# Order of the first loads: x blocks ahead of the q, k weight pieces, all four weight pieces on ScalarE's queue

## The chip, the core and the metric

The kernel runs on one core of a Trainium2 chip. The core has five engines that work side by side: TensorE (PE in the profile; its weight loads are PEld), VectorE (DVE), ScalarE (ACT), GpSimd (POOL) and SyncE (SP). Each works through its own instructions in order. Transfers between the chip's memory (HBM) and the core's on-chip memory are issued by SP, ACT or POOL as one instruction each, and are then carried out by 16 DMA engines. The metric is the device time of one execution in microseconds (us). Times in the text count from the first instruction of the profiled execution unless it says otherwise.

## What is computed

One transformer layer over 2048 positions of width 512 in bfloat16. Attention has 32 heads of width 16; each position looks at itself and at 7 earlier ones, 2 positions apart. The feed-forward part has a ReLU gate and width 1376.

```python
def _A_ref(x, wqkv, wo):
    H = 32; W, dil = 8, 2
    qkv = (x @ wqkv).reshape(B, S, 3, H, Dh)   # then q, k, v
    idx = pos[:, None] - off[None, :]          # off = arange(W) * dil
    logits = einsum("bhsd,bhswd->bhsw", q, kg) * Dh ** -0.5
    attn = softmax(where(mask, logits, -1e9))
    o = einsum("bhsw,bhswd->bhsd", attn, vg)
    return o @ wo

def _B_ref(x, W_gate, W_up, W_down):
    return (relu(x @ W_gate) * (x @ W_up)) @ W_down

h = x + _A_ref(_layernorm(x), A_wqkv, A_wo)
return h + _B_ref(_layernorm(h), B_W_gate, B_W_up, B_W_down)
```

## The kernel before

The 2048 positions are cut into four chunks of 512, and a chunk into four blocks of 128 positions. Block j of x lies in `x_sm[:, j, :]`, one position to a partition; below it is called xj (x0 to x3 are chunk 0, x4 to x7 chunk 1). The q and k weights lie in `wqk_sb` in four pieces of 128 input rows, `wqk_sb[:, 0..3, :]`, called w0 to w3; each is 256 KB, a block of x 128 KB. The v weights (`wv_sb`), the output weights (`wo_sb`) and the gate weights (`wgu_sb`) follow as larger transfers.

For chunk 0, each block goes its own way into the projections:

- DVE takes the statistics of the block (L467, aggregated by L470).
- ACT makes the reciprocal deviation of it with two activations (L480 logarithm, L484 exponential). They need ACT's function table, which is loaded by L326 in the setup.
- DVE normalizes the block (L515, into a `row` buffer).
- PE transposes it (L544, four matmuls against `identity`).
- ACT (L560), for block 1 DVE (L558), copies the transposed block into a `quad` buffer.
- PE multiplies it with the weights (L585): first the columns of block 0 and then of block 1 against w0 and w1 alone, then all columns against w2 and w3, then blocks 2 and 3.

Before that PE runs 77 matmuls on zeros (L428), and 8 more after the transposes of block 1 (L436). The order of all this on each engine is fixed by a table of ranks (`RANK`), which the change doesn't touch. Only the loads and constants in `setup()` stand outside of the table, ahead of everything else.

In `setup()` a loop issues the first eight loads (L319 to L325), alternating the queues of SP and ACT. On ACT the table load (L326) comes next. After the constants, SP issues w3 (L341), x5 to x7 (L343), the v weights (L344), the x blocks of chunks 2 and 3 (L346), the output weights (L348) and the gate weights (L349). A memset of one element on POOL (L340) stands ahead of w3, so that w3's DMA waits for POOL.

The framework gives each DMA of SP and ACT one of eight completion semaphores, called lanes (DMAHW0 to DMAHW7), in turn, in the order in which it expects the two queues to issue. A DMA that takes a lane again waits first, on the engine that issues it, until the DMA that had the lane has landed.

Of the kernel before, what the change touches and what calls it, by code (L numbers as in the profile page):

```python
# [201 lines left out]
def kernel(  # L202
# [11 lines left out]
    nc = tc.nc  # L214
    Bsz, S, D = A_x.shape
# [23 lines left out]
    BPC = CS // P  # L239
# [26 lines left out]
    wqk_sb = sb.tile([P, NT, 2 * D], BF16, name="wqk_sb")  # L266
# [50 lines left out]
    def setup():  # L317

        w3_r = A_wqkv.rearrange("(dt p) f -> p dt f", p=P)  # L319
        for q, n, j in ((nc.sync, "x", 0), (nc.scalar, "x", 1), (nc.scalar, "w", 0), (nc.sync, "x", 2), (nc.scalar, "w", 1),  # L320
                        (nc.sync, "x", 3), (nc.scalar, "w", 2), (nc.sync, "x", BPC)):
            if n == "x":
                q.dma_start(x_sm[:, j:j + 1, :], x_rows[:, j:j + 1, :])  # L323
            else:
                q.dma_start(wqk_sb[:, j:j + 1, :], w3_r[:, j:j + 1, 0:2 * D])  # L325
        nc.scalar.preload_act_table_set("natural_log_exp_and_others")  # L326
        V.memset(warm[:], 0.0)
        make_identity(nc, identity[:])
        nc.gpsimd.memset(eps_t[:, 0:1], EPS)
        nc.gpsimd.memset(eps_t[:, 1:2], EPS * D * D)  # L330
        nc.gpsimd.iota(ci[:], pattern=[[0, 1]], base=0, channel_multiplier=1)
        nc.gpsimd.iota(sel_i[:], pattern=[[1, H]], base=0, channel_multiplier=0)
        nc.gpsimd.iota(sp_i[:], pattern=[[1, H], [0, DQ]], base=0, channel_multiplier=0)
        nc.gpsimd.iota(sm_i, pattern=[[0, 4], [1, H]], base=0, channel_multiplier=0)
        nc.gpsimd.iota(mk_i[:], pattern=[[1, PADL]], base=0, channel_multiplier=0)
        nc.gpsimd.memset(kT[:, :, 0:PADL], 0.0)
        nc.gpsimd.memset(vT[:, :, 0:PADL], 0.0)


        nc.gpsimd.memset(wqk_sb[0:1, 3, 0:1], 0.0)  # L340
        nc.sync.dma_start(wqk_sb[:, 3:4, :], w3_r[:, 3:4, 0:2 * D])  # L341
        for j in range(BPC + 1, 2 * BPC):
            nc.sync.dma_start(x_sm[:, j:j + 1, :], x_rows[:, j:j + 1, :])  # L343
        nc.sync.dma_start(wv_sb[:], w3_r[:, :, 2 * D:3 * D])  # L344
        for tk in range(2, NCK):
            nc.sync.dma_start(x_sm[:, tk * BPC:(tk + 1) * BPC, :], x_rows[:, tk * BPC:(tk + 1) * BPC, :])  # L346

        nc.sync.dma_start(wo_sb[:], A_wo.rearrange("(p t) f -> p t f", t=NT))  # L348
        nc.sync.dma_start(wgu_sb[:, :, 0, :], B_W_gate.rearrange("(dt p) f -> p dt f", p=P))  # L349


        for n, (op, by) in enumerate(((ALU.arith_shift_right, 2), (ALU.bitwise_and, H - 1),
                                      (ALU.arith_shift_right, 5))):
            V.tensor_scalar(out=tmp[:, n:n + 1], in0=ci[:], scalar1=by, scalar2=None, op0=op)
        V.tensor_copy(out=cf[:, 0:3], in_=tmp[:])
        V.tensor_scalar(out=cf[:, 2:3], in0=cf[:, 2:3], scalar1=1.0 * DIL, scalar2=None, op0=ALU.mult)
        V.tensor_scalar(out=cf[:, 3:4], in0=cf[:, 2:3], scalar1=4.0 * DIL, scalar2=None, op0=ALU.add)
        V.tensor_scalar(out=sel[:], in0=sel_i[:], scalar1=cf[:, 0:1], scalar2=None, op0=ALU.is_equal)
        V.tensor_scalar(out=spread[:], in0=sp_i[:], scalar1=cf[:, 1:2], scalar2=None, op0=ALU.is_equal)
        V.tensor_scalar(out=same[:], in0=sm_i, scalar1=cf[:, 1:2], scalar2=None, op0=ALU.is_equal)  # L360
        for hf in range(2):
            V.tensor_scalar(out=mask[:, hf, :], in0=mk_i[:], scalar1=cf[:, 2 + hf:3 + hf],
                            scalar2=None, op0=ALU.is_ge)
# [204 lines left out]
    for tk in range(NCK):  # L568
# [339 lines left out]
        for f0 in range(0, NFT, 2):  # L908
# [70 lines left out]
            n, fs = len(fts), P if fts[-1] < NFF else FTAIL  # L979
# [66 lines left out]
    for o in plan.ops:  # L1046
        n = o.key[0] if o.key else ""
# [7 lines left out]
    with tc.manual_schedule():  # L1055
        setup()
        for op in todo:
            if op.fn is not None:
                op.fn()
# [35 lines left out]
```

## Time and profile before

| | |
|---|---|
| median of 3 runs | 192.64 us (191.8 to 192.98) |
| span of the profiled execution, first to last instruction | 190.2 us |
| median less that span | 2.4 us |
| PE busy | 185.1 us (97%) |
| DVE busy | 150.7 us (79%) |
| ACT busy | 113.5 us (60%) |
| HBM read | 8.42 MB |

Of the profiled execution the page gives the span; the time of a run also holds what lies around it. Busy shares are averages over stages with different limits: PE is busy nearly throughout, but in the first 40 us it often works with work from others that arrives just in time. How a stage is limited is read from the chain of work that ended last, which goes back from the last instruction, at each step to what released it.

### The profile page before, as it was taken

The numbers are of one execution on the slowest core, as the hardware profiler recorded it, in microseconds if no ns is written. First come the engines' busy times: TensorE is split into PE (matmuls) and PEld (weight loads), VectorE is DVE, ScalarE is ACT, GpSimd is POOL, SyncE is SP. The second block draws the span as 40 slices with busy tenths as digits, with TensorE's granted clock in tenths as the row PEclk, the third lists the DMA queues.
The fourth block names the chain that finished last, engine by engine and source line by source line (L and its number), as shares of the span: only waits on it lengthen the run. The fifth ranks groups of instructions, "written<-read, shape, count | busy, mean of one in ns | idle before, by whom it ended". The sixth has DMA issues, their size and how long they took to land.

```text
span 190.2 us, 3080 instructions
## 1 busy us (share of the span) xinstructions
PE 185.1 (97%) x1127; PEld 95.4 (50%) x1127; DVE 150.7 (79%) x231; ACT 113.5 (60%) x234; POOL 25.2 (13%) x47
## 2 busy tenths in 40 slices
PE   7799999999999999999999999999999999999993
PEld 7676555554444445544344464444454444455453
DVE  5899999999999999999999998998485712114324
ACT  2579999985467945762483795146466713358500
POOL 4000221400000004230033123027000000000000
PEclk9999999999999999999999999999999999999999
DMA  5999364993198858998438798779922211000503
GB/s 182 281 347 370 90 163 87 191 194 59 21 330 177 233 166 153 194 191 182 83 65 152 142 181 186 180 137 166 221 44 55 55 28 59 28 0 0 165 3 110
DMA packets 27743, 26.98 MB, mean 142 GB/s; under 512 B 14704, under 2 KB 23248, under 8 KB 27728
## 3 DMA queue, kind: packets, MB, share of 16 engines
q1 hardware_dynamic: 23696, 15.34, 29.7%
q0 software_dynamic: 3312, 10.49, 28.6%
q10 hardware_dynamic: 720, 0.95, 1.5%
q8 instruction: 9, 0.15, 0.3%
q14 instruction: 6, 0.05, 0.1%
HBM read 8.42 MB, written 2.10 MB: 55 GB/s over the span
## 4 chain that ended last, share of the span: by engine, by line
PE 82%; ACT 11%; DMA 3%; DVE 1%; issue 1%; SPq 0%
PE bank L954 37%; PE bank L1005 20%; PE bank L585 12%; PE bank L881 7%; ACT row L512 5%; DMA x_sm<-in_A_x_dram 3%; PE bank L921 3%; ACT quad L560 2%; ACT vT L593 2%; PE bank L642 2%; ACT quad L593 1%; PE bank L694 1%; ACT kT L593 1%; ACT ex L708 1%; SPq L323 0%
## 5 line engine op out<-in xcount | busy, mean ns | idle before, releaser
L954 PE MATMUL bank<-quad,wgu_sb 128*128 128x512 bf16 x320 | 72.3, 379 | 0.0
L954 PEld LDWEIGHTS <-wgu_sb 128*128 128x128 bf16 x320 | 30.9, 98 | 37.3 <-issue 1.7
L1005 PE MATMUL bank<-wd_sb,gT 128*128 128x512 bf16 (+3 forms) x198 | 39.7, 355 | 0.0
L958 ACT CAST up_sb<-bank 128x512 bf16<-128x512 f32 x40 | 23.1, 591 | 21.0 <-PE bank L954 14.9
L585 PE MATMUL bank<-quad,wqk_sb 128*128 128x512 bf16 (+2 forms) x176 | 30.4, 321 | 0.5 <-DVE quad L558 0.4
L961 ACT ACTIVATE gr<-bank 128x512 bf16<-128x512 f32 x40 | 23.3, 606 | 9.7 <-PE bank L954 8.2
L1005 PEld LDWEIGHTS <-gT 128*128 128x128 bf16 (+1 forms) x198 | 18.5, 98 | 19.7
L982 DVE TENSOR_TENSOR gT<-gr,up_sb 128x1024 bf16<-128x1024 bf16 x20 | 13.6, 686 | 14.4 <-PE bank L1005 7.0
L636 DVE TENSOR_TENSOR big<-quad,kT 128x4096 bf16<-128x4096 bf16 x11 | 24.8, 2279 | 0.0
L585 PEld LDWEIGHTS <-wqk_sb 128*128 128x128 bf16 x176 | 17.1, 113 | 11.4 <-issue 1.1
L800 DVE TENSOR_TENSOR big<-big,vT 128x4096 bf16<-128x4096 bf16 x9 | 20.4, 2281 | 0.0
L843 POOL DMA_DIRECT2D big<-big x13 | 11.6, 965 | 64.3 <-PE bank L954 32.6
L1013 DVE SCALAR_TENSOR_TENSOR row<-bank,iv,x_sm 128x512 bf16<-128x512 f32 (+2 forms) x10 | 6.3, 643 | 13.4 <-PE bank L1005 13.2
L457 ACT ACTIVATE junk<-x_sm,sm 128x512 bf16<-128x512 bf16 x16 | 11.6, 727 | 8.8 <-DVE x_sm L892 8.8
L585 PE MATMUL bank<-quad,wv_sb 128*128 128x512 bf16 x64 | 16.1, 380 | 0.2 <-ACT quad L560 0.2
L881 PE MATMUL bank<-wo_sb,quad 128*128 128x512 bf16 x64 | 15.0, 379 | 0.0
L892 DVE SCALAR_TENSOR_TENSOR x_sm<-x_sm,bank 128x512 bf16<-128x512 bf16 x16 | 10.8, 678 | 2.4 <-PE bank L881 2.4
L803 DVE TENSOR_TENSOR big<-big 128x1024 bf16<-128x1024 bf16 (+1 forms) x17 | 10.3, 622 | 1.6 <-DMA big<-big 1.4
L467 DVE BATCH_NORM_STATS2 st<-x_sm 128x6 f32<-128x512 bf16 x16 | 10.2, 679 | 1.1 <-DMA x_sm<-in_A_x_dram 1.1
L593 ACT CAST quad<-bank 128x512 bf16<-128x512 f32 x16 | 9.3, 594 | 2.5 <-PE bank L585 2.4
L593 ACT CAST kT<-bank 128x512 bf16<-128x512 f32 x16 | 9.3, 596 | 1.9 <-PE bank L585 1.0
L593 ACT CAST vT<-bank 128x512 bf16<-128x512 f32 x16 | 9.1, 610 | 2.1 <-PE bank L585 2.1
(80 smaller groups left out, 175.6 us busy)
## 6 DMA issues: line engine op xcount, KB each, us to landing
big<-big POOLq DMA_DIRECT2D x13, 512.0 KB, 5.2
big<-ex SPq DMA_DIRECT2D x20, 128.0 KB, 3.1
big<-ex POOLq DMA_DIRECT2D x12, 128.0 KB, 3.8
wgu_sb<-in_B_W_gate_dram SPq DMA_DIRECT2D x1, 1376.0 KB, 9.3
wgu_sb<-in_B_W_up_dram SPq DMA_DIRECT2D x2, 688.0 KB, 5.0
wd_sb<-in_B_W_down_dram SPq DMA_DIRECT2D x2, 640.0 KB, 5.7
x_sm<-in_A_x_dram SPq DMA_DIRECT2D x2, 512.0 KB, 6.2
wqk_sb<-wqk_sb POOLq DMA_DIRECT2D x2, 512.0 KB, 5.8
```

Of the source, the lines that this page charges most:

```text
L457: nc.scalar.activation(out=junk[:, j % 2, :], in_=h.t[:] if h else x_sm[:, tk * BPC + j, :], func=ACT.Square, bias=sm.t[:, j:j + 1], scale ...
L585: nc.tensor.matmul(mm.t[:, lo:hi], lhsT=wv_sb[:, dt, t:D:NT] if c == 2 else wqk_sb[:, dt, c * D + t:(c + 1) * D:NT], rhs=xnT.t[:, dt, lo:h ...
L593: nc.scalar.copy(out=o, in_=mm.t[:])
L636: V.tensor_tensor(out=pb.t[:].rearrange("p (t w) s -> p t w s", t=2), in0=q4, in1=k4, op=ALU.mult)
L800: V.tensor_tensor(out=mt.t[:], in0=ab.t[:], in1=v8, op=ALU.mult)
L843: nc.gpsimd.dma_start(mt.t[:, 0:4, :], mt.t[:, 4:8, :], accum_op=ALU.add)
L881: nc.tensor.matmul(od.t[:], lhsT=OT.t[:, t, j * P:(j + 1) * P], rhs=wo_sb[:, t, :], start=(t == 0), stop=(t == NT - 1 and tk not in RPE))
L954: nc.tensor.matmul(mm.t[:fs, lo:hi], lhsT=wgu_sb[:, dt, g, ft * P: ft * P + fs], rhs=hnT.t[:, dt, lo:hi], start=(dt == 0), stop=(dt == NT ...
L958: nc.scalar.copy(out=ub.t[:fs, i, :], in_=um.t[:fs, :])
L961: nc.scalar.activation(out=gr.t[:fs, i, :], in_=gm.t[:fs, :], func=ACT.Relu)
L982: V.tensor_tensor(out=gt.t[:fs, 0:n, :], in0=gr.t[:fs, 0:n, :], in1=ub.t[:fs, 0:n, :], op=ALU.mult)
L1005: nc.tensor.matmul(od.t[:, c0:c1], lhsT=gts[ft].t[:fs, ft % 2, j * P:(j + 1) * P], rhs=wd_sb[:fs, ft, c0:c1], start=(ft == 0), stop=(ft == ...
```

## The change

The first eight loads are issued in another order, and from other queues. x0 and x2 go first on SP's queue, x1 and x3 first on ACT's, and then all four weight pieces follow on ACT's. w3 and the memset ahead of it are gone from the later part of the setup, where SP now issues x4 to x7 (before, x4 was the last of the first eight).

```diff
-        for q, n, j in ((nc.sync, "x", 0), (nc.scalar, "x", 1), (nc.scalar, "w", 0), (nc.sync, "x", 2), (nc.scalar, "w", 1),
-                        (nc.sync, "x", 3), (nc.scalar, "w", 2), (nc.sync, "x", BPC)):
+        for q, n, j in ((nc.sync, "x", 0), (nc.scalar, "x", 1), (nc.sync, "x", 2), (nc.scalar, "x", 3), (nc.scalar, "w", 0),
+                        (nc.scalar, "w", 1), (nc.scalar, "w", 2), (nc.scalar, "w", 3)):
             if n == "x":
                 q.dma_start(x_sm[:, j:j + 1, :], x_rows[:, j:j + 1, :])
             else:
...
-        nc.gpsimd.memset(wqk_sb[0:1, 3, 0:1], 0.0)
-        nc.sync.dma_start(wqk_sb[:, 3:4, :], w3_r[:, 3:4, 0:2 * D])
-        for j in range(BPC + 1, 2 * BPC):
+        for j in range(BPC, 2 * BPC):
             nc.sync.dma_start(x_sm[:, j:j + 1, :], x_rows[:, j:j + 1, :])
```

Every line of the kernel behind L340 has a number lower by 2 in the changed kernel. The order on PE and DVE is the same as before; on POOL the memset is gone. What changes is on ACT and SP. ACT's first instructions before (a wait in brackets names the semaphore):

```order
L323 DMA x_sm<-in_A_x_dram 128x512
L325 DMA wqk_sb<-in_A_wqkv_dram 128x1024 x3
L326 ACT_TABLE_LOAD
L480 ACTIVATE rs_129<-mv_117,eps_t 128x1 [waits DVE_49,Pool_49]
L484 ACTIVATE rs_129<-rs_129 128x1 [waits Activation_49]
```

And in the changed kernel, where L478 is the L480 of before:

```order
L323 DMA x_sm<-in_A_x_dram 128x512 x2
L325 DMA wqk_sb<-in_A_wqkv_dram 128x1024 x2
L325 DMA wqk_sb<-in_A_wqkv_dram 128x1024 [waits DMAHW2_49]
L325 DMA wqk_sb<-in_A_wqkv_dram 128x1024 [waits DMAHW4_49]
L326 ACT_TABLE_LOAD
L478 ACTIVATE rs_129<-mv_117,eps_t 128x1 [waits DVE_49,Pool_49]
```

ACT issues six DMAs instead of four ahead of its table load, and the last two wait for lanes. SP's first instructions before:

```order
L323 DMA x_sm<-in_A_x_dram 128x512 x4
L341 DMA wqk_sb<-in_A_wqkv_dram 128x1024 [waits DMAHW0_49,Pool_49]
L343 DMA x_sm<-in_A_x_dram 128x512 [waits DMAHW1_49]
L343 DMA x_sm<-in_A_x_dram 128x512 [waits DMAHW2_49]
L343 DMA x_sm<-in_A_x_dram 128x512 [waits DMAHW3_49]
L344 DMA wv_sb<-in_A_wqkv_dram 128x4x512 [waits DMAHW4_49]
```

And SP's in the changed kernel:

```order
L323 DMA x_sm<-in_A_x_dram 128x512 x2
L341 DMA x_sm<-in_A_x_dram 128x512 x2
L341 DMA x_sm<-in_A_x_dram 128x512 [waits DMAHW0_49]
L341 DMA x_sm<-in_A_x_dram 128x512 [waits DMAHW1_49]
L342 DMA wv_sb<-in_A_wqkv_dram 128x4x512 [waits DMAHW3_49]
```

x4 and x5 are issued without a wait, and the other loads wait for other lanes than before. Which load has which lane is seen from those who wait for it to use the data; on PE the first projections of the changed kernel stand as follows (LDWEIGHTS of `wqk_sb` reads w0 first and then w1):

```order
L434 LDWEIGHTS warm
L434 MATMUL bank_138<-warm 128x128
L583 LDWEIGHTS wqk_sb [waits DMAHW4_49]
L583 MATMUL bank_141<-quad_79,wqk_sb 128x128 [waits Activation_49]
L583 LDWEIGHTS wqk_sb [waits DMAHW7_49]
```

Lane 4 is w0's and lane 7 is w1's there. DVE's statistics wait for lane 1 (x0), 0 (x1), 3 (x2), 2 (x3), 5 (x4) and 6 (x5), read in the same way.

## The prediction

> **What bounds the kernel now.** Read in this order: the page's chain of work that ended last, the same chain in order of time, the timeline of the first 17 us, then the landings of the first DMAs. The page names PE for 82% of the chain, with a small part for a DMA of x.
>
> ```profile
> span 190.2 us, 3080 instructions
> ...
> PE 82%; ACT 11%; DMA 3%; DVE 1%; issue 1%; SPq 0%
> ```
>
> In order of time (start, duration, what) the chain begins with a transfer:
>
> ```profile
> 1.70 5.60 DMA x_sm<-in_A_x_dram
> ...
> 7.33 0.71 DVE st L467
> ...
> 8.92 0.40 PE bank L544 x4
> ...
> 10.48 5.54 PE bank L585 x54
> ...
> 16.52 2.93 ACT row L512 x4
> ...
> 37.70 7.07 PE bank L585 x32
> ```
>
> Up to 7.30 us the end waits for x block 3 (issued at 1.70). Then come its statistics on DVE, its transposes, from 10.48 to 16.02 the q, k projections on PE, from 16.52 to 37.7 ACT, and from 37.70 PE without a gap. Nothing there has slack, so a shift of the chain before 10.48 us arrives in full at the end. The question is what the new load order does to block 3's way into PE. The timeline of the engines on that way (start, duration, engine, line):
>
> ```profile
> 0.74 0.40 ACTq L323 DMA_DIRECT2D x_sm<-in_A_x_dram  x1
> ...
> 1.17 1.44 ACTq L325 DMA_DIRECT2D wqk_sb<-in_A_wqkv_dram  x3
> ...
> 2.64 1.28 ACT L326 ACT_TABLE_LOAD   x1 [2.64 <-issue]
> ...
> 4.72 0.30 ACT L480 ACTIVATE rs<-mv,eps_t 128x1 f32<-128x1 f32 x1 [0.80 <-DVE mv L470]
> ...
> 5.33 0.38 DVE L515 TENSOR_SCALAR row<-x_sm,mv,rs 128x512 bf16<-128x512 bf16 x1
> 5.63 0.69 DVE L467 BATCH_NORM_STATS2 st<-x_sm 128x6 f32<-128x512 bf16 x1
> ...
> 5.77 0.40 PE L544 MATMUL bank<-identity,row 128*128 128x128 bf16 x4
> 6.23 0.40 DVE L515 TENSOR_SCALAR row<-x_sm,mv,rs 128x512 bf16<-128x512 bf16 x1
> 6.54 0.18 DVE L470 BATCH_NORM_AGGREGATE mv<-st 128x2 f32<-128x6 f32 x1
> ...
> 6.92 0.61 PE L436 MATMUL bank<-warm 128*128 128x128 bf16 x8
> ...
> 7.33 0.69 DVE L467 BATCH_NORM_STATS2 st<-x_sm 128x6 f32<-128x512 bf16 x1 [0.61 <-DMA x_sm<-in_A_x_dram]
> ...
> 7.37 0.83 PE L585 MATMUL bank<-quad,wqk_sb 128*128 128x128 bf16 x12
> ...
> 8.15 0.39 DVE L558 COPY quad<-bank 128x512 bf16<-128x512 bf16 x1
> ```
>
> The reader is to see ACT's own order: three weight DMAs issued until 2.61, the table load to 3.92, and then an engine that is free before its first activation (L480, block 0) is needed at 4.72. DVE's L515 for block 0 (5.33) waits for that activation's chain, and every later DVE instruction stands behind it: statistics of block 2 (5.63), of block 3 (7.33, idle 0.61 us for the DMA), the copy L558 that lets PE go on.
>
> **Part 1: ACT's queue.** In the changed kernel ACT issues x1, x3, w0, w1, then w2 with a wait on lane DMAHW2 and w3 with a wait on lane DMAHW4, and only then the table load. By the rows of the order, lane 2 is x3's and lane 4 is w0's (PE's first LDWEIGHTS of wqk_sb waits for it too). Before, none of ACT's DMAs had a wait. That such a wait holds the issuing engine is seen on SP, whose fifth DMA (w3, ninth of both queues) has one:
>
> ```profile
> SPq L341 <- DMA x_sm<-in_A_x_dram: 0.9, 1, 0.9
> 3.60 0.33 SPq L341 DMA_DIRECT2D wqk_sb<-in_A_wqkv_dram  x1
> x_sm<-in_A_x_dram ACTq DMA_DIRECT2D x1, 128.0 KB, 2.8
> wqk_sb<-in_A_wqkv_dram ACTq DMA_DIRECT2D x1, 256.0 KB, 3.3
> x_sm<-in_A_x_dram SPq DMA_DIRECT2D x1, 128.0 KB, 3.4
> x_sm<-in_A_x_dram SPq DMA_DIRECT2D x1, 128.0 KB, 5.6
> ```
>
> The four lines of DMA issues give the time from issue to landing of x1 (0.74 + 2.8 = 3.5), w0 (1.17 + 3.3 = 4.5), x2 (1.21 + 3.4 = 4.6) and x3 (1.70 + 5.6 = 7.3). SP stood 0.9 us and issued at 3.60, 0.1 after x1 landed. So ACT's table load now starts after w0 has landed, and all that ACT owes to layernorm stands behind it.
>
> When does w0 land? Third on its queue, behind x1 and x3, and beside x0, x2 and x4 of SP's queue: 4 x 128 + 256 + 128 KB = 0.917 MB. What the DMA engines moved before (last number, GB/s):
>
> ```profile
> 1.00:2.00 1.00, 1.00 (x19) 1.00 (x20) 0.46 (x4) 0.00 (x0) 0.98 (x7) 1.00 0.13 38
> 2.00:3.00 1.00, 1.00 (x24) 1.00 (x22) 0.93 (x7) 0.36 (x1) 0.52 (x6) 1.00 0.92 291
> 3.00:4.00 1.00, 1.00 (x23) 1.00 (x21) 0.52 (x3) 0.92 (x1) 0.00 (x0) 1.00 0.97 341
> 4.00:5.00 1.00, 1.00 (x16) 0.94 (x14) 0.97 (x3) 0.28 (x1) 0.00 (x0) 1.00 0.91 274
> ```
>
> That is 0.038 + 0.291 + 0.341 + 0.274 = 0.944 MB at 5.0 us, so 0.917 at 4.9. Before, w0 and x2 were complete at x0 to x2 + w0 = 0.655 MB, reached at 3.95, and landed 0.5 to 0.7 later. So w0 lands near 5.5. Lower bound: 4.6, x2's landing in second place with less data before it. Upper bound: 7.3, x3's, third on its queue beside w1. I take 5.5, nearer to the lower, because x3 had 0.13 MB more before it and a gap between data and landing that only that place shows.
>
> From there: 0.1 to resume, 0.48 for w3's issue (1.44 / 3), 1.28 for the table load: the first L480 can start at 7.37. Now the steps as measured, from the start of block 0's L480 (4.72): L515 at +0.61, statistics of block 2 at +0.91, L515 of block 1 0.60 later (5.63 to 6.23), the aggregate of block 2 0.31 after that (6.54), and 0.10 more to the statistics of block 3: +1.92. Before, these stood at 7.33. From there on all steps are the same instructions in the same order, so the shift is 7.37 + 1.92 - 7.33 = 1.96, say **+2.0 us**. Bounds: w0 at 4.6 gives +1.1, at 7.3 gives +3.8. The change gains only if L480 starts before 5.41, that is if w0 lands before 3.55; x1, first on the queue, landed at 3.5.
>
> **Part 2: what the x blocks gain.** x2 and x3 come second on their queues: near 4.2, at most 4.6. Nobody can use that: DVE reaches their statistics at 8.3 and 9.3. The 3 us by which x3 lands earlier are worth nothing once ACT is the later one.
>
> **Part 3: PE's pause.** Before, the 77 warming matmuls fill PE to 5.8 us, where block 0's transposes (5.77) follow. These now start at 7.37 + 1.05 = 8.42, a pause of 2.6 us. What a pause does to the granted clock is seen at the end of the profile, and what a low clock does at the start (the third number from the right is PEclk; for the first 5 us it reads 1.00, so the pace is taken from the counts):
>
> ```profile
> 4.50:5.10 0.60, 0.60 (x8) 0.60 (x8) 0.60 (x2) 0.35 (x2) 0.00 (x0) 1.00 0.90 314
> 5.30:5.60 0.30, 0.30 (x9) 0.30 (x6) 0.30 (x2) 0.15 (x1) 0.00 (x0) 1.00 0.85 277
> 187.00:188.00 1.00, 0.29 (x6) 0.12 (x3) 0.55 (x2) 0.00 (x0) 0.00 (x0) 1.00 0.80 261
> 189.00:189.70 0.70, 0.00 (x0) 0.00 (x0) 0.00 (x0) 0.00 (x0) 0.00 (x0) 0.89 0.00 0
> 189.70:190.20 0.50, 0.00 (x0) 0.00 (x0) 0.00 (x0) 0.00 (x0) 0.00 (x0) 0.50 0.00 0
> ```
>
> PE's last work ends at 187.29. In 189.00 to 189.70 the mean clock is 0.89, and then 0.50: it fell at about 189.55, 2.3 us after the last matmul. At the start, 0.60 us hold 8 matmuls of the warming row at 4.5 and 0.30 us hold 9 at 5.3: PE started at about half pace and came up near 5.2, some 4 us after its first matmul. So a 2.6 us pause is likely enough to drop the clock, and PE would then work at half pace for some 3 to 4 us. In that stretch lie 8 fills (L436, 0.61 us), 12 first matmuls of q, k (0.83) and 2 more, each 0.055 (the four more matmuls of the second row take 0.22): 22 x 0.055 = 1.2 more. At full pace they end at L480 + 2.2 (6.92 - 4.72) + 1.2 = 3.4, and block 2's transposes, which stand behind them on PE, can start at 1.92 + 8.92 - 7.33 = 3.5 after L480. 0.1 is to spare, so **+1.1 us**. Bounds: 0, if the clock holds; 2, if half pace lasts into the 5.54 us of L585.
>
> [...]
>
> **Part 4: the rest.** w2 and w3 are now issued near 4.3 and 5.6, where w3 had 3.60. PE asks for w1 at 6.92 + 0.45 - 4.72 = 2.65 after L480 (10.0), and for w2 and w3 behind the transposes of block 3, L480 + 4.2 or more (11.6). The longest landing of a piece decides:
>
> ```profile
> wqk_sb<-in_A_wqkv_dram ACTq DMA_DIRECT2D x3, 256.0 KB, 5.4
> wqk_sb<-in_A_wqkv_dram SPq DMA_DIRECT2D x1, 256.0 KB, 5.2
> ```
>
> 5.4 (median) and 5.2 put w1, issued near 2.1, at 7.5 and w3 at 10.8: nothing, covered by 0.8 us at the least; without that cover, as when L480 comes early, w3 would be the next to be late. x4 to x7, wv and the later loads are issued earlier on SP (x4 at 1.70, wv after x2 instead of after x3) and land earlier; the first reader of x4, DVE, comes later than before. Their cost is the company that they give to w0, counted above with x4. The memset removed on POOL cost 0.09 us under an 18 us pause, so nothing:
>
> ```profile
> 2.42 0.09 POOL L340 MEMSET wqk_sb<- 1x1 bf16 x1
> ...
> 20.96 1.30 POOL L768 DMA_DIRECT2D big<-ex  x2 [18.45 <-DVE ex L711]
> ```
>
> **Sum.** +2.0 + 1.1 = +3.1: the profiled span goes from 190.2 to about 193.3. The runs' median, 192.64, lies 2.4 above the span; I leave that unchanged: 195.7 us.
>
> **Rivals.**
> Clock holds: ACT late as above, but PE keeps full pace. For it speaks that PE is idle only 0.3 us longer than at the drop in the profile, and that one drop fixes no threshold. 192.64 + 2.0 = 194.6, from +1.1 to +2.9 (193.7 to 195.5). [...]
> w0 lands late, as x3 did third on its queue (7.3): 192.64 + 3.8 + 1.1 = 197.5. For it: 5.6 us between issue and landing at that place. Against: less data ahead.
> Not slower: the waits on ACT do not bind, so x3's early landing is what counts. ACT would issue six DMAs to 0.74 + 0.40 + 5 x 0.48 = 3.5, end the table load at 4.8, and L480 would start 0.1 later than before; block 3's statistics then come at 4.8 + 1.92 = 6.7 instead of 7.33: -0.6, or 192.0. It decides only if w0 lands before 3.55 or lane 4 is free before that. Against it is the order of the changed program and the 4.5 at which w0 landed with one block of x ahead, not two.
>
> **How the numbers follow.** ACT late with a clock drop: 0.52 (its own range 194.9 to 196.6). Clock holds: 0.25. w0 late: 0.15. Not slower: 0.03; between it and the forecast, w0 near 4.6 with the clock held (193.7): 0.05. The likeliest gives 195.7. The range 193.8 to 197.3 leaves out the two early cases and part of the late one. A measurement of this kernel tells about 1% (1.9 us) from no change. Faster: 0.02, for a gain larger than the last rival's 0.6. Same: most of that rival, the early case and half of clock holds, 0.20. Slower: the rest, 0.78.
>
> **What would show it.** In the profile of the changed kernel: ACT's third weight DMA is issued near 4.3 and the fourth near 5.6; the table load near 6.1 instead of 2.64; L480 near 7.4; block 0's transposes near 8.4 after a pause of PE; a PEclk of 0.5 for some 3 us from about 8.6; block 3's statistics near 9.3 with no wait for a DMA; the step that starts PE's main run (10.48 before) near 13.5; from there the same times shifted by one amount. A table load at 3.5, or a first L480 before 5.4, would make the prediction wrong in sign; a shift that shrinks between 16 and 38 us would show slack that I say is not there.

## The result and the profile after

| | before | after |
|---|---|---|
| median of 4 runs each, us | 192.22 (191.43 to 192.98) | 197.72 (196.83 to 197.73) |
| ratio, 95% interval | | 1.0279 (1.0237 to 1.0322) |
| span of the profiled execution, us | 190.2 | 196.0 |

The changed kernel is slower by 5.5 us in the median and by 5.8 in the profiled execution. The forecast was 195.7, its range ended at 197.3. A run more than 1.5% above the fastest of its kernel counts in the medians and ranges below, but not in a ratio and its interval. Below, "shift" is the start of an instruction less the start of the same instruction in the profile before.

First the page of the changed kernel: its span, and the granted clock in 40 slices of 4.9 us.

```profile
span 196.0 us, 3055 instructions
...
PEclk9958999999999999999999999999999999999999
```

The low clock lies in the third and fourth slice (9.8 to 19.6 us); then it stays full to the end of the span. Next the timeline on block 3's way (start, duration, engine, line; in brackets the idle time before and who ended it):

```profile
1.67 5.80 ACTq L325 DMA_DIRECT2D wqk_sb<-in_A_wqkv_dram  x4
...
7.50 1.28 ACT L326 ACT_TABLE_LOAD   x1 [7.50 <-DMA wqk_sb<-in_A_wqkv_dram]
8.80 0.29 ACT L478 ACTIVATE rs<-mv,eps_t 128x1 f32<-128x1 f32 x1
9.36 0.41 DVE L513 TENSOR_SCALAR row<-x_sm,mv,rs 128x512 bf16<-128x512 bf16 x1 [3.82 <-ACT rs L482]
9.83 0.61 PE L542 MATMUL bank<-identity,row 128*128 128x128 bf16 x4 [3.61 <-DVE row L513]
10.69 0.67 DVE L465 BATCH_NORM_STATS2 st<-x_sm 128x6 f32<-128x512 bf16 x1
...
16.62 0.58 ACT L591 CAST quad<-bank 128x512 bf16<-128x512 f32 x1 [1.02 <-PE bank L583]
```

ACT is held with issuing its weight DMAs until 7.47: the third goes out at 4.12, just after x3 landed (4.10), the fourth at 7.13, just after w0 (7.11). The table load then comes at 7.50 (before: 2.64), though nothing on its way needs the weights. DVE waits 3.82 us for ACT, PE pauses 3.61 us. Block 3's statistics stand at 10.69, 3.36 later than before (7.33), without a wait for x. The first evacuation of the projections stands at 16.62. In the timeline of the kernel before it stood here:

```profile
10.90 0.58 ACT L593 CAST quad<-bank 128x512 bf16<-128x512 f32 x1 [0.47 <-PE bank L585]
```

That is a shift of 5.72: 2.36 more came in between, on PE. The stretches of the changed kernel (length, PE busy with its matmuls; the last three numbers are granted clock, DMA share and GB/s):

```profile
1.00:2.00 1.00, 1.00 (x19) 1.00 (x20) 0.46 (x4) 0.00 (x0) 0.98 (x7) 1.00 0.27 35
2.00:3.00 1.00, 1.00 (x23) 1.00 (x22) 0.93 (x7) 0.00 (x0) 0.48 (x5) 1.00 0.90 237
3.00:4.00 1.00, 1.00 (x24) 1.00 (x22) 0.39 (x3) 0.00 (x0) 0.00 (x0) 1.00 1.01 310
4.00:5.00 1.00, 1.00 (x16) 0.94 (x14) 0.97 (x3) 0.00 (x0) 0.00 (x0) 1.00 0.80 236
5.00:6.00 1.00, 1.00 (x12) 0.95 (x9) 0.51 (x2) 0.00 (x0) 0.00 (x0) 1.00 0.87 307
...
9.00:10.00 1.00, 0.17 (x2) 0.17 (x3) 0.64 (x2) 0.68 (x4) 0.00 (x0) 0.76 1.13 377
10.00:13.00 3.00, 2.69 (x26) 2.43 (x25) 2.97 (x9) 1.48 (x5) 0.00 (x0) 0.50 1.08 351
13.00:16.00 3.00, 3.00 (x27) 2.73 (x26) 2.25 (x8) 1.17 (x2) 0.00 (x0) 0.50 1.03 395
16.00:17.00 1.00, 1.00 (x15) 0.98 (x14) 0.00 (x0) 0.38 (x1) 0.00 (x0) 0.83 1.03 402
```

The clock is at half from about 9.5 to 16.3, 6.8 us in which PE hardly rests once it is back at 9.83. From there the chain of work that ended last (start, duration, what) has the steps of before, each at one distance:

```profile
22.24 2.93 ACT row L510 x4
...
43.41 7.07 PE bank L583 x32
```

Before, these stood at 16.52 and 37.70: +5.72 and +5.71. The span grew by 5.8. So in these two profiles nothing of the early shift was absorbed, and nothing added.

### The profile page after: what moved, and what is told of

It is laid out like the page before. It is cut to its first block, busy times and chain, and to the rows that moved or that the text cites. A ratio compares the mean times of both kernels' runs of the same rounds, so it can differ in the third digit from the quotient of the medians.

```text
span 196.0 us, 3055 instructions
## 1 busy us (share of the span) xinstructions
PE 186.9 (95%) x1108; PEld 98.1 (50%) x1127; DVE 150.8 (77%) x231; ACT 113.4 (58%) x234; POOL 25.2 (13%) x46
## 3 DMA queue, kind: packets, MB, share of 16 engines
q10 hardware_dynamic: 1008, 1.34, 2.3%
## 4 chain that ended last, share of the span: by engine, by line
PE 82%; ACT 11%; DMA 4%; issue 1%; DVE 1%; SPq 0%
PE bank L952 35%; PE bank L1003 19%; PE bank L583 13%; PE bank L879 7%; ACT row L510 4%; PE bank L919 3%; DMA wv_sb<-in_A_wqkv_dram 3%; ACT quad L558 2%; ACT vT L591 2%; PE bank L640 1%; DMA x_sm<-in_A_x_dram 1%; ACT quad L591 1%; PE bank L692 1%; ACT kT L591 1%; PE bank L542 1%
## 5 line engine op out<-in xcount | busy, mean ns | idle before, releaser
L583 PE MATMUL bank<-quad,wqk_sb 128*128 128x512 bf16 (+2 forms) x172 | 31.5, 336 | 0.2
L583 PEld LDWEIGHTS <-wqk_sb 128*128 128x128 bf16 x176 | 18.5, 119 | 11.0 <-issue 0.4
L583 PE MATMUL bank<-quad,wv_sb 128*128 128x512 bf16 x62 | 15.9, 380 | 0.3 <-ACT quad L558 0.2
L649 DVE TENSOR_TENSOR big<-quad,kT 128x2048 bf16<-128x2048 bf16 x8 | 9.3, 1218 | 2.5 <-ACT kT L591 2.5
L766 POOL DMA_DIRECT2D big<-ex x12 | 6.8, 585 | 29.1 <-DVE ex L709 24.2
```

Of the source, the lines that this page charges most:

```text
L583: nc.tensor.matmul(mm.t[:, lo:hi], lhsT=wv_sb[:, dt, t:D:NT] if c == 2 else wqk_sb[:, dt, c * D + t:(c + 1) * D:NT], rhs=xnT.t[:, dt, lo:h ...
```

## The experiments

Three questions: is the wait on ACT the cause (e1, e4, e5, e6, e8), what does the half pace cost (e2, e7, e10 to e12), and why do equal early shifts end as different totals (e9, e12 to e16). In each batch the kernel before ran on the same chip, with medians of 191.5 to 192.2; a ratio is against those runs. Where a time from a profile is given, it is of one execution.

**e1, the waits on ACT taken away by holding x4 to x7.** One memset into x4's place, behind the constants on POOL, makes SP's later loads come later; the framework then gives lanes so that none of ACT's DMAs waits (its four weight pieces are issued from 1.68 to 3.58). The new order of the first eight loads stays.

```diff
+        nc.gpsimd.memset(x_sm[0:1, BPC, 0:1], 0.0)
         for j in range(BPC, 2 * BPC):
```

> The changed kernel with one more instruction: a one-element memset of x4's place on POOL ahead of x4's load, so that x4 to x7 count as issued after w3 and none of ACT's six loads has a wait on a lane. Theory (the hold of ACT by the lane waits costs all): table load at 3.5 to 4.8 us, first L480 near 4.9, the whole loss gone: 192.2 us, between 191.2 and 193.0. Rival 1 (the new load order itself, w pieces behind two x blocks, costs a part beside the hold): projections wait for w0 or w1, 193.5 to 195. Rival 2 (the hold is not the cause): 197 or more.

Measured: 192.23 (191.14 to 192.82, 10 runs), ratio 0.9997 (0.9973 to 1.0021). The timeline of this kernel:

```profile
3.61 1.28 ACT L326 ACT_TABLE_LOAD   x1 [3.61 <-issue]
...
6.80 0.66 DVE L466 BATCH_NORM_STATS2 st<-x_sm 128x6 f32<-128x512 bf16 x1
```

The whole loss is gone. Block 3 even comes 0.53 earlier than before (6.80 against 7.33), and the first evacuation at 10.35, 0.55 earlier; that lead is lost again between 66 and 141 us. Putting x ahead of the weights is harmless here. This run also takes x4 to x7 away from the first weights; e4 and e5 show that the wait on ACT is what costs.

**e4, the four weights on SP's queue.** SP waits for lanes there, where nothing but loads stands behind (x4 to x7 are issued from 3.68 to 5.44, the v weights at 6.18).

```diff
-        ... (nc.scalar, "w", 0), (nc.scalar, "w", 1), (nc.scalar, "w", 2), (nc.scalar, "w", 3)):
+        ... (nc.sync, "w", 0), (nc.sync, "w", 1), (nc.sync, "w", 2), (nc.sync, "w", 3)):
```

> The changed kernel with all four weight pieces on SP's queue instead of ACT's, behind x0 and x2; ACT issues x1 and x3 alone, no load of the first eight has a wait. Theory: table load at 1.7 to 2.9 us, first L480 near 4.7, block 3's statistics near 6.6 instead of 7.3 (before the change); w0 and w1 then decide. If they land by 7 us: 191.6, if as late as third and fourth places did (7.1 and 8.1): 192.2; between 190.9 and 192.8. Rival (one queue alone moves the weights slower than two): w1 and w3 late, 193.5 or more.

Measured: 191.96 (191.59 to 192.51, 10 runs), ratio 0.9987 (0.9963 to 1.0011). Its table load stands at 1.67, the first evacuation at 9.96, 0.94 earlier than before. The chain of work shows one place where the lead shrinks (to 0.45 at 50 us; it is gone by 95):

```profile
36.41 9.65 DMA big<-big
46.08 1.36 DVE big L801 x3
```

This accumulating DMA, the fourth of its group, took 8.07 us in the kernel before.

**e5, the kernel before with such a wait.** A copy of one element of w1 makes ACT wait for that piece ahead of the table load; the loads are in the old order.

```diff
+        nc.scalar.copy(out=junk[0:1, 0, 0:1], in_=wqk_sb[0:1, 1, 0:1])
         nc.scalar.preload_act_table_set("natural_log_exp_and_others")
```

> The kernel before with one more instruction on ACT ahead of its table load: a copy of one element of w1 that has to wait until w1 has landed (7.1 us). The load order is that of before. Theory (a late table load on ACT and the pause of PE make the whole loss, whatever the load order): first L480 near 8.7, pause of PE near 4 us, clock down for one or two spells, 197.5 us, between 195.5 and 198.5. Rival (the changed order of the loads makes a good part of the loss): below 195.

Measured: 196.96 (196.01 to 197.58, 4 runs), ratio 1.0243 (1.0195 to 1.0292). The timeline:

```profile
7.07 0.19 ACT L326 COPY junk<-wqk_sb 1x1 bf16<-1x1 bf16 x1 [3.15 <-DMA wqk_sb<-in_A_wqkv_dram]
7.28 1.28 ACT L327 ACT_TABLE_LOAD   x1
...
10.48 0.66 DVE L468 BATCH_NORM_STATS2 st<-x_sm 128x6 f32<-128x512 bf16 x1
```

Two stretches of it (the numbers as above):

```profile
9.00:12.00 3.00, 2.08 (x19) 1.82 (x20) 2.82 (x9) 1.98 (x8) 0.00 (x0) 0.50 0.92 306
12.00:15.00 3.00, 3.00 (x33) 3.00 (x32) 3.00 (x9) 0.95 (x2) 0.00 (x0) 0.62 1.08 388
```

Block 3's statistics shift by 3.15, PE pauses 4.29 us, the clock is at half for 6.8 us (7.5 to 14.3), the first evacuation comes at 15.70 (+4.80), and the profiled span is 195.3 (+5.1). A wait on ACT of nearly this length makes nearly the whole loss without the new load order. What the half pace does to whole runs is less clear: the other three runs had a mean clock of 0.991, 0.991 and 1.000 (0.982 in the profiled run; the half pace at the start doesn't count in it: in the changed kernel the later 6.8 us at half alone make 0.983 of its 196.0 us, and 0.983 is its mean), and took 196.01, 196.72 and 197.58 us.

**e6, the table load between w1 and w2.** In this kernel the last weight DMA waits for x4 and not for w0.

```diff
+            if (n, j) == ("w", 2):
+                nc.scalar.preload_act_table_set("natural_log_exp_and_others")
```

> The changed kernel with the table load moved ahead of ACT's third weight DMA; the last one still waits, by the new order of lanes for x4 (which landed at 7.3 us in the changed kernel), and L480's counterpart stands behind it. Theory (what stands behind the held DMA is late, and by its own length less if the table load is out of it): first L480 near 7.7 instead of 8.8, block 3's statistics near 9.7, PE's pause 3 us; 1.1 us less than the changed kernel with the same spell of half pace, 196.6 us; 194.5 if the clock holds; between 194.2 and 197.0. Rival (the table load alone is the trouble): 192.5 or less.

Measured: 194.51 (193.86 to 195.37, 4 runs), ratio 1.0141 (1.0112 to 1.017). The first activation still stands behind a DMA that waits:

```profile
6.72 0.29 ACT L479 ACTIVATE rs<-mv,eps_t 128x1 f32<-128x1 f32 x1 [2.80 <-DMA x_sm<-in_A_x_dram]
...
11.51 1.84 PE L584 MATMUL bank<-quad,wqk_sb 128*128 128x256 bf16 x21 [0.38 <-DMA wqk_sb<-in_A_wqkv_dram]
```

Half of the loss stays. It is not the table load that matters, but everything of ACT behind the waiting DMA. PE's pause is 1.54 us, and the clock holds in the profile (mean 1.000); but the three other runs, 0.5 to 1.5 us longer, have a mean clock of 0.990 to 0.991, which is some 3.5 us at half (0.009 of 193 us, divided by 0.5). The second row is new: with ACT early, PE waits for w3.

**e8, x5 held, x4 not** (the memset of e1 with `BPC + 1`).

> The changed kernel with a one-element memset of x5's place on POOL ahead of x5's load: x4 alone is issued early beside w0, and the only wait left on ACT is w3's for x1 (3.5 us). For the time theory and rival say the same, 191.8 to 193.2, with L480 near 5.4. It is run for the landing of w0. Theory (x blocks on SP's queue beside the weights make w0 late; 5.9 us without them, 7.1 and 7.7 with x4 and x5): x4 alone gives 6.3 to 7.1. Rival (w0 was late by chance, or for the hold of w2 and w3): 5.9 or less.

Measured: 192.77 in one run. w0 landed at 6.73. It is third on ACT's queue in six other profiles too: at 5.88 in e1 (no block of chunk 1 beside it), and at 6.83, 6.96, 7.01, 7.11 and 7.70 in e11, e6, e12, the changed kernel and e2 (x4 and x5 beside it). The last five are spread over 0.9 us, so one profile of e8 doesn't set x4 alone apart from them; e1 does stand apart. In none of the seven does w0 land at the 5.5 of the forecast.

**e2, PE's pause filled.** 60 more warming matmuls in the changed kernel: `NWARM` from (62, 15) to (62, 75).

> The changed kernel with 60 more matmuls on zeros in the warming row of PE, 3.3 us at 0.055, so that PE has hardly a pause before block 0's transposes; ACT is held as before. Theory (hold of ACT 3.4 us, half pace after the pause of PE 2.3 us): clock 1.00 throughout, 2.3 us less than the changed kernel, 195.4 us, between 194.8 and 196.0. Rival (half pace is hidden behind ACT and DVE): no change, 197.7. The fill itself must not end later than 9.8 us.

Measured: 196.81 (196.52 to 198.95, 4 runs), ratio 1.0264 (1.0199 to 1.0329); a miss, and not told apart from the changed kernel. The clock is full from block 0's transposes on (1.00 in the stretches from 9 to 16 us). The timeline and the chain of work:

```profile
8.08 1.28 ACT L326 ACT_TABLE_LOAD   x1 [8.08 <-DMA wqk_sb<-in_A_wqkv_dram]
...
11.28 0.66 DVE L465 BATCH_NORM_STATS2 st<-x_sm 128x6 f32<-128x512 bf16 x1
```

```profile
14.40 5.54 PE bank L583 x54
...
60.67 2.82 DMA quad<-row
63.62 8.79 PE bank L952 x40
```

Up to 60 us the shift is 3.92, what the late w0 (7.70 here) alone makes: 14.40 - 10.48. The half pace is gone. Then PE waits for transposing DMAs and the shift grows to 4.9.

**e10, e11, the same in e5 and e6** (`NWARM` (62, 65) in e5, (62, 38) in e6).

> The kernel before with the waiting copy on ACT (as in the run named e5_before_wait) and 50 more matmuls in PE's warming row, 2.8 us, so that PE has a pause of about 1 us instead of 4.3; first L480 again near 8.6. Theory (hold and half pace add up; half pace was 4.79 - 3.12 = 1.7 us of that run's shift): mean clock 1.00 in every run, main run of PE shifted by 3.1 to 3.3, 195.2 us, between 194.6 and 196.0. Rival (half pace costs nothing beside the hold, and other waits make the rest): 196.5 or more.

> The changed kernel with the table load ahead of the third weight DMA (as in the run named e6_table_mid) and 23 more matmuls in PE's warming row, 1.3 us, which close most of PE's pause there. In that run the profile kept a clock of 1.00 and the three others had 0.99. Theory (a spell of half pace after a pause of 1.5 us comes in some executions and costs 0.5 to 1.5 us in them): all runs at 1.00 and 193.9 us, between 193.2 and 194.4. Rival (the spread of those runs has other causes): 194.5, like that run.

Measured: 198.14 (196.11 to 200.23, 4 runs), ratio 1.0313 (1.0239 to 1.0386), and 196.9 (196.17 to 197.85, 4 runs), ratio 1.03 (1.026 to 1.034). Both missed, and upwards: they are no faster than the kernels without the filling, or slower. Two of e10's runs, the two longest, still have a mean clock of 0.991. In the profile of e10 the shift is 3.34 up to 42 us, as the wait alone makes it. Then DVE waits, and later PE (1.26 us at 64.65):

```profile
43.91 0.69 DVE L804 TENSOR_TENSOR big<-big 128x1024 bf16<-128x1024 bf16 x1 [0.85 <-DMA big<-big]
```

In e11 the same wait is 1.23 us, at 43.25.

**e7, the kernel before without warming** (`NWARM` (1, 0)), to price half pace by itself.

> The kernel before with one warming matmul instead of 77 (and none of the 15 wider ones), so that PE comes to block 0's transposes at half pace, with nothing else changed: the price of the low clock alone. Theory (half pace in this stretch is not hidden, as the changed kernel's 2.35 us say): clock 0.50 until one or two spells of 3.4 us after 5.8 us, 193.4 to 195.0 us, 194.4 if it lasts as long behind the first transposes as in the changed kernel. Rival (half pace is hidden behind DVE's and ACT's waits for x3): 192.2 to 192.6.

Measured: 194.56 for the profiled execution, ratio 1.0147 (1.01 to 1.0194) over the runs. By its matmuls PE is at half pace to about 9.6 us (the four of a transpose take 0.61 us at 5.73 and 0.39 at 9.93). x3 landed 0.37 earlier, the first evacuation comes 0.55 later: 0.92 for the half pace. But the span is 2.6 longer, because DVE waits 1.34 us for an accumulating DMA at 41.61 and PE twice 0.8 to 1.0 us later on. That the total came out near the expected 194.4 is luck: the half pace made a third of it. So the kernels with another number of warming matmuls (e2, e7, e10, e11) have waits for DMAs between 40 and 65 us, 0.43 us in e2 and 0.8 to 1.3 in the others; of those with the same number, e4 and e8 alone have one there, of 0.5 to 0.6.

**e9, the kernel before once more.**

> The kernel before, unchanged, for a second profile of it. If the waits of PE and DVE for DMAs between 45 and 150 us, in which two experiments lost a lead of 0.6 and 0.95 us, come at other places from run to run, this profile has other gaps there than the first one, some tenths of a us in all, and a span of 189.8 to 190.8. If they are fixed, it has the same two gaps of DVE (130.2 and 141.0 us) and none of PE.

Measured: 192.35, span 190.5. x3 landed at 6.73 by itself, the first evacuation came at 10.33, and that lead of 0.57 was gone by 100 us. So in this kernel, as in e1, a lead of half a microsecond wasn't worth anything, and the time before doesn't hang on the late x3 of its first profile.

**What the kernels with waits have in common.** The trace also holds the packets of a queue named instruction. Those of 16 KB come eight or nine times and take 0.88 to 1.82 us each, half of them under 0.97. That they load PE's instructions is inferred: more or fewer matmuls ahead move them against the rest. Times (us) of accumulating DMAs of chunk 0 in which one starts, and of the first of the four transposing DMAs near 55 to 64 where one starts among them, beside the same DMA in kernels where none does:

```
kernel   packet at   DMA, from issue to landing     its time   without
e7       34.46       first,  32.73 to 39.04           6.31       4.61
e10      38.08       first,  35.52 to 41.36           5.84       4.61
e11      40.53       second, 35.60 to 43.23           7.63       6.15
e4       44.04       fourth, 36.41 to 46.06           9.65       7.59 (e2 alone)
before   44.78       fourth, 37.20 to 45.27           8.07       7.59 (e2 alone)
e2       57.81       transpose, 55.98 to 62.09        6.11       5.10 to 5.39
e7       57.32       transpose, 54.02 to 60.39        6.36       5.10 to 5.39
e10      60.08       transpose, 56.33 to 63.12        6.79       5.10 to 5.39
```

**e12, the pause filled with as many instructions as before.** The changed kernel with fewer but longer warming matmuls, as many in all as before, so that the code stays in place.

```diff
-    NWARM, NFILL = (62, 15), (8, 0, 0)
+    NWARM, NFILL = (53, 24), (8, 0, 0)
...
-            nc.tensor.matmul(wb.t[0:m, 0:m], lhsT=warm[:, 0:m], rhs=warm[:, 0:m], start=True, stop=True)
+            n, r = (m, warm) if k < NWARM[0] else (D, zero)
+            nc.tensor.matmul(wb.t[0:m, 0:n], lhsT=warm[:, 0:m], rhs=r[:, 0:n], start=True, stop=True)
```

> The changed kernel with PE's pause filled by longer warming matmuls (24 of 512 columns instead of 15 of 128) and as many instructions on PE as before; every warming matmul works on zeros, one more memset on VectorE makes them. Theory A (the waits at 42 to 140 us in the bridged kernels come from PE's code: the trace has packets of 16 KB of the queue named instruction, about 0.95 us each, and more PE instructions move them into accumulating and transposing DMAs): the packets stand where they stand in the changed kernel, less the half pace; full clock, shift at 15 us as table load + 3.2 - 7.33 gives, +3.4 to +3.9, and the same at the end; span 193.6 to 194.2, median 196.0 (195.6 to 196.5). Theory B (those waits are chance, or come with every bridged pause): DVE waits 0.8 or more for big<-big near 42 us or PE for quad<-row near 63 us, shift grows to +4.9 or more, median 196.8 or more.

Measured: 195.99 (195.38 to 196.61, 6 runs), ratio 1.0221 (1.0183 to 1.0259). Full clock (1.00 in the stretches from 9 to 16 us); the shift is 3.23 up to 44 us and 3.95 at the end. The total is as theory A has it, the course not quite: the shift begins below its 3.4 to 3.9, and 0.6 was added at the fourth accumulating DMA, which took 9.65 us, as in e4, with a packet at 48.06 in it.

**e13, the kernel before with 146 fewer instructions on PE, in the same time.**

```diff
-    NWARM, NFILL = (62, 15), (8, 0, 0)
+    NWARM, NFILL = (0, 10), (2, 0, 0)
```

(and the matmul of e12, for the fills too)

> The kernel before with fewer and longer warming matmuls (10 of 512 columns instead of 77, 2 instead of 8 fills): PE is busy in the same stretch, but has 146 instructions less (73 matmuls with their weight loads) ahead of the rest. Theory A: the packet of PE's code that comes at 44.78 in the kernel before comes at 32 to 37, inside the first accumulating DMA (32.2 to 36.8 before); that DMA takes 5.8 to 6.3 us instead of 4.6, DVE's L803 waits 0.9 to 1.5 for it, and the time is +0.9 to +1.5: 193.7 (193.1 to 194.3). Theory B: where the code lies makes no difference, 192.2 (191.6 to 192.8), accumulating DMAs of 4.6 and 6.2.

Measured: 198.87 (197.68 to 201.28, 6 runs), ratio 1.0352 (1.0309 to 1.0395); a miss for both theories. The profile is of the longest run; the others are 1.9 to 3.6 us shorter, so not all of its waits are theirs, but all six runs are at least 4.6 us longer than any run of the kernel before beside them. The shift is 0.10 up to 31 us: the start of the kernel is as good as before. What a stretch of 0.1 us at 29.1 holds, by queue (packets, MB, share of 16 engines' time; the 104.1% of 1.6 us are the 1.67 us of one packet), and the chain of work from there:

```profile
q8 instruction: 1, 0.02, 104.1%
q1 hardware_dynamic: 74, 0.02, 89.1%
```

```profile
26.41 5.19 DMA quad<-row
31.60 0.02 issue
31.63 0.30 ACT row L515
31.93 3.40 DMA quad<-row
```

The four transposing DMAs there took 5.19, 4.87, 4.13 and 3.40 us, where they took 2.91, 2.44, 3.25 and 2.78 before. PE waits 1.39 us, and its clock falls, at 35.88 for 3.4 us and again at 134.87 (the mean is 0.983). The stretches at the first place, and PE's row after the second, where a packet came at 125.82:

```profile
34.00:36.00 2.00, 0.62 (x3) 0.38 (x4) 2.00 (x2) 2.00 (x5) 0.28 (x1) 0.97 1.03 186
36.00:38.00 2.00, 2.00 (x6) 0.69 (x5) 2.00 (x3) 1.57 (x3) 1.23 (x2) 0.50 1.08 207
```

```profile
135.18 2.29 PE L957 MATMUL bank<-quad,wgu_sb 128*128 128x512 bf16 x5 [3.89 <-DMA quad<-row]
```

Theory A had the packet in the first accumulating DMA, at a price of 0.9 to 1.5; it came earlier, in the transposes, and cost far more. That fewer instructions on PE, in the same time, made the total 7 us longer is shown as far as one control goes: e12, made from the changed kernel, has the same memset and the same kind of long matmuls, and none of these waits. That the packets are the means is argued from where they start, not a thing that was switched on and off by itself.

**e14, e15, e16, a few instructions fewer.** e4 with `NWARM` (58, 15) and (52, 15), and the kernel before with (58, 15).

> All four weight pieces on SP's queue (as e4), and 58 instead of 62 of the first warming matmuls: 8 instructions less on PE, so that each packet of PE's code is asked for 8 instructions later. In e4 one came at 44.04, while the fourth accumulating DMA ran (9.65 us instead of 8.05), and DVE waited 0.54 behind it. Theory A: the packet comes at 44.7 to 45.2, after that DMA has landed (44.5); the DMA takes 8.1, DVE does not wait there, and some 0.4 to 0.6 of e4's lead of 0.95 stays to 60 us; 191.4 (190.9 to 191.9), where e4 had 191.96. Theory B: 191.96 as e4, the wait of 0.5 stays.

> As the run above with 52: 20 instructions less. Theory A: the packet comes near 46, the fourth accumulating DMA takes 8.1 us, but the packet that came at 87.25 comes near 89.5, between four transposing DMAs (88.4 to 94.8 in e4), which then take longer than 2.5 us; PE waits for them. 191.4 to 193. Theory B: 191.96.

> The kernel before with 58 instead of 62 first warming matmuls, nothing else. Theory A: in the kernel before the packet came at 44.78, 0.5 before the fourth accumulating DMA landed; 8 instructions later it comes near 45.6, after it. Nothing to win there, 192.2 (191.6 to 192.8), by either theory; a control for the 8 instructions.

Measured, 12 runs each: 191.23, ratio 0.9966 (0.9945 to 0.9986); 191.15, ratio 0.9951 (0.9928 to 0.9974); 191.83, ratio 0.9992 (0.9968 to 1.0016). In e14 and e15 the fourth accumulating DMA takes 8.07 and 8.12 us and e4's lead stays, 0.82 and 0.79 up to 95 us. So e14's total is as theory A has it, e15's is below its 191.4 to 193, e16's is as both have it, and the reason of theory A fails in detail: the packets came at 43.93 and 44.05, within the DMA and not later than in e4 (44.04), and e15's packet of 87.25 did not move into the transposes. Over all 17 profiles, a packet starts in the fourth accumulating DMA of twelve at 43.9 to 50.5 us; nine of these DMAs took 8.04 to 8.17 us, the changed kernel's among them, and three (e4, e8, e12) 9.65 to 9.69. So a packet in it doesn't decide by itself, and what does is open. These two are the fastest kernels of the study, by 0.3 to 0.5% against before; against e4 itself, which ran in another batch, they were not measured.

## Why the prediction was right in kind and too small

- **ACT's queue, the mechanism: right.** The third and fourth weight DMA waited for x3 and for w0, the table load came behind them, and block 3's statistics came 1.89 us after the first activation (1.92 in the forecast). e1 and e4 remove the wait and the loss, e5 makes a like wait and nearly the same loss.
- **"So w0 lands near 5.5": the step that failed.** It landed at 7.11. The amount of data was right: 0.035 + 0.237 + 0.310 + 0.236 is 0.818 MB at 5.0, and 0.917 at 5.3. The lag from there to the landing was taken from second places (0.5 to 0.7) and was 1.8. One row for the third place was x3's: in the kernel before, 0.944 MB at 5.0 and the stretch below put its 1.05 MB at 5.3, and it landed at 7.3, 2.0 later.

```profile
5.00:6.00 1.00, 1.00 (x16) 0.86 (x13) 0.97 (x4) 0.72 (x4) 0.00 (x0) 1.00 0.92 316
```

  The forecast saw that gap, called it one "that only that place shows", and then didn't use it though w0 took that place. A nearer row still was w1's in the kernel before: third on ACT's queue, of the same size and issued at the same 1.67 as w0 is now. The DMA issues of a stretch around 1.67 have this line word for word in both kernels (from issue to landing, in us):

```profile
wqk_sb<-in_A_wqkv_dram ACTq DMA_DIRECT2D x1, 256.0 KB, 5.4
```

  Part 4 of the forecast takes this 5.4, which it calls the longest (w2 had 5.9), for w1 and not for w0; it would have given 7.1. Why the landing comes so late after the mean data is open. The trace has sixteen steps for each DMA's completion: w0's came in from 4.74 to 7.11, eight of them by 5.34 and twelve by 5.97, and the wait ends with the last. In e2 fifteen were in by 5.76, and the last came at 7.70.

  The 1.6 us of later landing came out as 1.4 more of shift: +3.36 instead of +1.96. The rival "w0 lands late" was what happened. That its 197.5 came so near to 197.72 is partly luck: its terms were 3.8 and 1.1, the trace has 3.36 and 2.36.
- **PE's pause: right in kind, half the size; the second term that failed.** The clock fell, against the rival "clock holds". But the pause was 3.61 us and not 2.6, as w0 was late, and half pace lasted 6.8 us, not "some 3 to 4". It then reached into the 5.54 us of L585 (L583 here), the case of the forecast's upper bound (2), and cost 2.36 instead of 1.1, more than that bound. The trace has 3.41 us from the clock's rise (6.10) to its fall (9.51) and then 6.83 at half (to 16.34); in e5 the clock was at half for 6.8, too. The 2.3 us to the drop that the forecast took from the end of the kernel is no fixed delay: in the changed kernel the clock fell 4.2 us after the last matmul (197.24 and 193.03), and over the ends of the 15 profiles that record it, it ran from 2.0 to 4.9 us. Nor does the length of a pause alone tell what the clock does: in e13 it fell at 35.88 after a pause of 1.39 us, and e6's profile kept it over 1.54.
- **The x blocks' earlier landing worth nothing: right.** e1 has them early and gains nothing in the median.
- **The rest at nothing: right here.** w1 landed at 8.07, w3 at 12.15, and PE didn't wait for them. The next in line was named rightly: in e6, with ACT early, PE waits for w3.
- **"A shift of the chain before 10.48 us arrives in full at the end": right for this change, not a rule.** It was carried within 0.1 us in the changed kernel. But leads of 0.55 to 0.95 (e1, e4, e9) are lost between 30 and 141 us, mostly in waits for DMAs, and e2, e10 and e11 add 1 to 2 us there.
- **The sum.** 1.40 too little for w0 and 1.25 for the half pace make the +3.1 of the forecast the +5.72 of the trace. The forecast's time also has 2.4 us for what lies around the span; of the runs whose span is on record, all lie 1.7 to 2.0 above it (197.73 and 196.0 here). So the span of 193.3 was 2.7 too small, and the time only 2.0. What the half pace costs in whole runs is not as sharp: e12, without it, has a ratio of 1.0221 where the changed kernel has 1.0279, which is 1.1 us, and the intervals overlap; e2, without it too, is not told apart from the changed kernel.

## What to carry to other kernels

A DMA that waited for a completion lane held everything behind it on the engine that issues it (ACT's table load came at 7.50 instead of 2.64): put the setup that others need (here the table load) and the first activations ahead of such DMAs, or issue these from an engine with nothing else to do. When a landing is estimated, take the time from issue to landing of a transfer of the same size at the same place of the same queue (here 5.41 us for w1 before, 5.44 for w0), and more than one profile: in the seven profiles with the load order of before, x3 landed at 6.73 to 7.66. When an experiment changes the number of instructions on an engine, keep a control with the same number in the same time, since 146 fewer instructions on PE in the same time made this kernel 3.5% slower (e13).

## What the runs showed of the hardware that was not expected

- The third transfer of a queue landed 1.8 us (w0) and 2.0 us (x3 before) after the DMA engines had moved as much as it and all ahead of it, the second 0.5 to 0.7 after. The place alone doesn't fix this: for w0 it was 0.9 in e1 and 2.4 in e2, for x3 1.2 in e9.
- The clock was at half for 6.8 us after the pauses of 3.61 us and, in e5, 4.29. Of the first 3.4 us of that PE was busy for 2.8 and 1.0, of the second 3.4 all the time, and only then did the clock rise. In e5 it had fallen 2.2 us after the last warming matmul, with PE still busy for 1.3 of the 3.4 us before the fall. A short pause did it as well: one of 1.39 us in e13, and, judged by their mean clock alone, those of three runs of e6 (0.990 to 0.991), whose profiled run paused 1.54 and kept its clock.
- The queue named instruction is busy together with the kernel's own transfers: in e13's stretch of 0.1 us above with one packet beside 74 of theirs. Its packets of 16 KB took 0.88 to 1.82 us, and the DMAs of the table above in which one starts took 0.5 to 2.1 us longer than without; how a packet would make a DMA longer was not shown. The first two transposing DMAs of e13 took 2.3 and 2.4 us longer, which goes beyond the 1.67 us of the packet there, and no run here shows why.
